# Conversion steps regrouped by slot, and the first units' exchanged x moved to transfers, in a threshold-attention and bilinear-FFN kernel

## The chip, the cores and the metric

The kernel runs on one core of a Trainium2 chip. The metric is the device time of one execution in microseconds (us). A core has a matrix engine (TensorE, PE in the profile, with PEld for its weight loads), VectorE (DVE), ScalarE (ACT), GpSimd (POOL) and SyncE (SP). SP issues most transfers; each engine works through its own instructions in order and waits for others by semaphores.

## The reference

Eight batches of eight heads attend over 576 positions with head size 64. Scores more than tau below a row's maximum are dropped. The outputs of the heads, side by side, are the 512 columns of x, and 4608 rows of x go through a bilinear FFN.

```python
scores = scale * np.matmul(q, k.transpose(0, 1, 3, 2))          # (8, 8, 576, 576)
thresh = np.max(scores, axis=-1, keepdims=True) - tau
scores = np.where(scores >= thresh, scores, -1000000000.0)
attn = np.exp(scores - np.max(scores, axis=-1, keepdims=True))
attn = attn / (np.sum(attn, axis=-1, keepdims=True) + 1e-09)
x = np.matmul(attn, v)                                          # then (B*S, H*D) = (4608, 512)
out = ((x @ w_a) * (x @ w_b)) @ w_out                           # d_ff = 1536
```

The weights arrive as 64-bit floats. The kernel reads them as pairs of 32-bit words and makes 32-bit floats of them itself.

## The kernel before, in words

**Slots.** Heads are taken in pairs; a batch has four pairs, and there are 32. A unit is 128 query rows of a pair (the fifth unit of a pair is the tail of 64 rows). One main loop goes over `g`, one unit per slot. In batch 0 the order is different from the rest: first rows 0 to 127 of all four pairs (units of slots 0 to 3), then rows 128 to 255 (slots 4 to 7), then the others. The whole program is one order written out by this loop, and `keep_order` fixes it for every engine.

**A unit.** `scores` has TensorE multiply (L312) into two PSUM tiles, VectorE take the maximum of each (`mx`, L319) and Pool make `bias` (L320) and `thr` (L321) of them. `weigh` has ACT take the exponential (L332) and VectorE multiply by the mask and sum (L336). `reciprocal` follows. For the first eight units, `diagonals` makes diagonal matrices of the reciprocals (L362), and in the next slot `turn_pe` transposes and scales on TensorE in two products: the main part (L374), which ACT copies out (L376), and the tail (L380), which ACT copies out too (L382). For these eight units, `weighted_unit`, two slots after the unit, multiplies with v (L449) and joins two halves into x (`xT`, L438 on ACT and L439 on VectorE). From slot 8 on, units are normalised on ACT (L355), transposed in blocks on VectorE (L401) and turned by a round trip through memory instead.

**The exchange.** The FFN needs x also with its two groups of 64 partitions swapped, `xS`. `exchange` (L459) copies it: on VectorE for the first eight units, on Pool for all later blocks.

**The FFN.** It runs as a generator in blocks of 256 rows; `advance` issues a number of its columns per portion of a slot (`PACE_EARLY` until slot 8, `PACE` after). A block has six steps `f` with w_a and w_b (L530) of 256 columns each, then the products with w_out (L550). The first block is ready piecemeal: its steps 0 and 1 are split into halves of 128 columns. A step is issued only when `state["converted"]` weight pieces are there and, in the first block, `state["rows"]` units of x.

**Weight conversion.** The weights are 36 pieces of 128 by 512: 24 of w_a and w_b, then 12 of w_out. `load_weights` keeps up to five raw pieces (512 KB each) loaded, in buffers of the tag "xT", of which there are seven and which x shares. A piece takes six operations:

| function | engine | line | what |
|---|---|---|---|
| convert_first | ACT | L213, L214 | absolute value of the upper word; scaling of the lower word |
| convert_clamp | POOL | L220 | clamp to the range |
| convert_sign | DVE | L226 | sign bit of the upper word joined into the lower part; frees the raw buffer |
| convert_shift | DVE | L232 | shift left by 3 |
| convert_add | POOL | L237 | integer addition of both parts |

`early[g]` lists the pieces that slot `g` starts: two each, three in slots 4 to 9. The first of a slot and the others ("late") are treated differently, by `of`: the first goes through first and clamp after the masks, sign after the normalisation or diagonals, and shift at the slot's end, and is added at the top of the next slot. The late ones start at the slot's end, are clamped and signed before the masks of the next slot, and shifted and added after its reciprocal. So on VectorE the six steps of a slot lie in four places, and on Pool the additions in two.

**Start.** SP first loads tau, from which VectorE makes five scalars (L270 to L275), then rows of q (k's on ACT's queue), raw weights and v. The rows lie in two buffers of tag "tb" (9 KB per partition) and two of tag "xT". In slots 0 to 2 `prep_pe` transposes them on TensorE (L296) and `prep_copy` copies them out (L301). Tag "tb" is needed again from slot 9, by the blocks of L401.

Of the kernel before, what the change touches and what calls it, by code (L numbers as in the profile page):

```python
# [11 lines left out]
U32 = mybir.dt.uint32  # L12
# [12 lines left out]
XT_BUFS = 7  # L25
# [25 lines left out]
def kernel(  # L51
# [36 lines left out]
    nc = tc.nc  # L88
    B, H, S, D = q.shape
    P = 128  # L90
    Q = 32
    DM = H * D
    DFF = w_a.shape[1]
    HP = H // 2
    NT = 4
# [84 lines left out]
    NPIECES = len(pieces)  # L180
    raws, stages = {}, {}
    state = {"loaded": 0, "converted": 0, "rows": 0}

    def load_weights(limit, engine=nc.sync):

        while len(raws) < limit and state["loaded"] < NPIECES:
            n = state["loaded"]
            raw = work.tile([P, CW, 2], U32, tag="xT", bufs=XT_BUFS, name="raw")
            src = pieces[n][1]
# [44 lines left out]
    def convert_add(n):  # L234
        if n in stages:
            top, low = pieces[n][0].bitcast(I32), stages.pop(n).bitcast(I32)
            nc.gpsimd.tensor_tensor(top, top, low, op=ALU.add)  # L237
            state["converted"] = n + 1


    scalars = const.tile([P, 8], FP32, name="scalars")
    tau_sb = scalars[:, 5:6]
    nc.sync.dma_start(tau_sb, tau.to_broadcast([P, 1]))
    rooms = []
# [7 lines left out]
    load_rows(1, "q", rooms[2])  # L252
    load_rows(1, "k", rooms[3], nc.scalar)
    load_weights(2)
    load_rows(2, "q", rooms[4])
# [109 lines left out]
    def turn_pe(i, u):  # L365
# [12 lines left out]
        for j, w in enumerate(ws):  # L378
            c = MAIN * (1 - j)
            nc.tensor.matmul(tp[TAIL * j:TAIL * (j + 1)], w[:, c:c + TAIL], dg[:, j],  # L380
                             start=True, stop=True)
        nc.scalar.copy(wT[:, NT], tp)  # L382

# [77 lines left out]
    def exchange_blocks():  # L461
        while complete:
# [4 lines left out]
            blocks.append(((x, xs), what))  # L467

    def weighted_unit(i, u):

# [5 lines left out]
        join(x_of[b, 0][:, hp, u * P:(u + 1) * P], pv[:, 0], pv[:, 1])  # L476
        exchange(x_of[b, 0], state["xs"], hp, u * P, (u + 1) * P, nc.vector)
        if hp == HP - 1:
            state["rows"] = u + 1
            if u == 0:  # L480
                blocks.append(((x_of[b, 0], state["xs"]), ("first", b, 0)))

# [22 lines left out]
    def ffn(xT, what):  # L505
# [7 lines left out]
        if kind == "first":  # L513
            steps = [(f, c, c + P) for c in (0, P) for f in range(n)] + steps[n:]
        for f, c0, c1 in steps:
# [110 lines left out]
    for g in range(NPIECES):  # L626
        size = min(3 if 4 <= g < 10 else 2, NPIECES - n)
        early[g] = list(range(n, n + size))
        n += size
    def of(g, late):  # L630

        return early.get(g, [])[1:] if late else early.get(g, [])[0:1]

    for g in range(len(units) + PV_LAG):
# [12 lines left out]
        if 2 <= g < BY_PE + 2:  # L647
            weighted_unit(*units[g - 2])
            running["owed"] -= (NSLOT + 1) // 2 * P
        for n in of(g - 1, False):  # L650
            convert_add(n)
        for n in of(g - 1, True):
            convert_clamp(n)
        if g < 3:
            prep_copy(*prep_pe(g + 1, "q"))
        for n in of(g - 1, True):
            convert_sign(n)
        load_weights(5 if g < 10 else 4)
        if g > BY_PE and g <= len(units):
# [13 lines left out]
        if g > BY_PE:  # L673
            advance(PORTIONS[1] * pace)
            n = g - PV_LAG
            if BY_PE <= n < len(units) and part(*units[n]):
                make_room()
                weighted(*part(*units[n]))
                running["owed"] -= (NSLOT + 1) // 2 * width(*part(*units[n]))
        for n in of(g, False):  # L680
            convert_first(n)
            convert_clamp(n)
        if here:
            reciprocal(i, u, nc.scalar if converting else nc.vector)
        for n in of(g - 1, True):
            convert_shift(n)
        for n in of(g - 1, True):
            convert_add(n)
        if here and g < BY_PE:
            diagonals(i, u)  # L690
        elif here:
            normalise(i, u)
        for n in of(g, False):
            convert_sign(n)
        load_weights(5 if g < 10 else 4)
# [8 lines left out]
        advance((PORTIONS[2] if g > BY_PE else sum(PORTIONS[:3])) * pace)  # L704
        for n in of(g, True):
            convert_first(n)
        for n in of(g, False):
            convert_shift(n)
        advance(PORTIONS[3] * pace)
# [37 lines left out]
```

## Time and profile before

| what | us |
|---|---|
| median of 3 runs | 1541.02 (1540.39 to 1543.94) |
| the profiled execution | 1543.14, span 1541.0 |
| PE busy in the span | 1484.0 (96%) |
| DVE busy | 878.4 (57%) |
| ACT busy | 590.0 (38%) |
| POOL busy | 261.6 (17%) |

The profile is of one execution. Busy is the time in which an engine worked on something; PE's ends are modelled, so a busy PE need not be at its peak. PE's granted clock (PEclk) is given in tenths or as a share of full speed. In groups, "x36" is a count, and the time in brackets is idle time of the engine ahead of an instruction, with what ended it. A matmul of 32-bit floats is recorded as two. The conversion of weights lies in the first 165 us of the span.

### The profile page before, as it was taken

What the parts mean: (1) busy time and instruction counts of PE and PEld (TensorE: products, weight loads), DVE (VectorE), ACT (ScalarE), POOL (GpSimd) and SP (SyncE); (2) the same over time, 40 slices, a digit from 0 to 9 for tenths busy, and PEclk for the clock granted to TensorE, in tenths of its full rate; (3) what the DMA queues carried; (4) which work ended last, traced back from release to release, by engine and by line L of the source; (5) the groups of instructions that cost most, each with busy time, mean ns of one, the idle gap of its engine ahead of it and who ended that gap; (6) DMA issues with size and microseconds to landing.
All of it is one profiled execution on the core that took longest, in us unless ns stands there. A gap on an engine that the chain in (4) does not pass through costs nothing.

```text
span 1541.0 us, 51117 instructions
## 1 busy us (share of the span) xinstructions
PE 1484.0 (96%) x22640; PEld 1145.4 (74%) x22640; DVE 878.4 (57%) x1844; ACT 590.0 (38%) x935; POOL 261.6 (17%) x662
## 2 busy tenths in 40 slices
PE   5778999999999999999999999999999999999998
PEld 3666786675777576778777787877777879798886
DVE  5999676567656765665545754576645665510010
ACT  4767354334433443443323433344433443410000
POOL 2666211101110111020100101011110111110000
PEclk8889999999999999999999999999999999999999
DMA  9658888679868876795547966588748876430000
GB/s 202 150 139 226 173 174 194 163 152 188 192 148 155 185 182 150 147 193 133 123 100 145 190 149 138 119 173 177 171 95 159 182 173 125 123 84 15 2 15 15
DMA packets 624557, 220.38 MB, mean 143 GB/s; under 512 B 542928, under 2 KB 612048, under 8 KB 624336
## 3 DMA queue, kind: packets, MB, share of 16 engines
q1 hardware_dynamic: 621968, 216.52, 64.1%
q8 instruction: 178, 2.92, 0.8%
q10 hardware_dynamic: 2368, 0.59, 0.2%
q14 instruction: 43, 0.35, 0.1%
HBM read 127.40 MB, written 89.65 MB: 141 GB/s over the span
## 4 chain that ended last, share of the span: by engine, by line
PE 88%; DVE 5%; SPq 2%; ACT 1%; issue 1%; DMA 1%; POOL 0%; POOLq 0%; DVEq 0%; ACTq 0%
PE pab L530 45%; PE po L550 24%; PE pv L449 9%; PE sc L312 9%; DVE low L226 1%; SPq L140 1%; DVE w L336 1%; DVE mx L319 1%; SPq L411 1%; DMA raw<-in_moe_w_b_dram 0%; PE tp L374 0%; DVE tb L401 0%; SPq L423 0%; DVE wb_sb L232 0%; DVE wo_sb L232 0%
## 5 line engine op out<-in xcount | busy, mean ns | idle before, releaser
L550 PE MATMUL po<-wo_sb,h 64*64 64x512 f32 x3456 | 424.3, 589 | 0.0
L550 PEld LDWEIGHTS po<-wo_sb,h 64*64 64x64 f32 x3456 | 222.8, 133 | 137.6 <-issue 79.7
L319 DVE TENSOR_REDUCE mx<-sc 128x1 f32<-128x576 f32 x288 | 205.0, 748 | 201.4 <-PE sc L312 201.2
L332 ACT ACTIVATE w<-sc,bias,scalars 128x576 f32<-128x576 f32 x288 | 226.8, 827 | 190.2 <-POOL bias L320 178.7
L312 PE MATMUL sc<-kT,qT 64*64 64x288 f32 x2304 | 264.1, 412 | 21.5 <-DVE w L336 9.8
L530 PE MATMUL pab<-xS,wa_sb 64*64 64x256 f32 (+1 forms) x3520 | 278.7, 376 | 3.3 <-POOL xS L459 3.3
L530 PE MATMUL pab<-xS,wb_sb 64*64 64x256 f32 (+1 forms) x3520 | 279.4, 377 | 2.5 <-issue 2.5
L355 ACT ACTIVATE w<-w,rcp 128x576 f32<-128x576 f32 x272 | 197.7, 768 | 182.9 <-DVE rcp L349 182.7
L320 POOL TENSOR_SCALAR bias<-mx,scalars 128x1 f32<-128x1 f32 x288 | 85.5, 297 | 1050.3 <-DVE mx L319 624.5
L530 PE MATMUL pab<-xT,wb_sb 64*64 64x256 f32 (+1 forms) x3136 | 250.9, 377 | 0.5 <-DVE h L538 0.5
L530 PE MATMUL pab<-xT,wa_sb 64*64 64x256 f32 (+1 forms) x3136 | 243.4, 373 | 4.4 <-DVE xT L439 3.5
L336 DVE SCALAR_TENSOR_TENSOR w<-sc,thr,w 128x576 f32<-128x576 f32 x288 | 222.4, 804 | 20.5 <-ACT w L332 17.8
L530 PEld LDWEIGHTS pab<-xS,wa_sb 64*64 64x64 f32 x3520 | 193.4, 134 | 33.6 <-POOL xS L459 9.8
L530 PEld LDWEIGHTS pab<-xS,wb_sb 64*64 64x64 f32 x3520 | 196.5, 135 | 27.9 <-issue 3.1
L312 PEld LDWEIGHTS sc<-kT,qT 64*64 64x64 f32 x2304 | 148.2, 134 | 71.6 <-issue 18.3
L530 PEld LDWEIGHTS pab<-xT,wa_sb 64*64 64x64 f32 x3136 | 170.4, 133 | 30.4 <-DVE xT L439 3.8
L530 PEld LDWEIGHTS pab<-xT,wb_sb 64*64 64x64 f32 x3136 | 173.5, 135 | 24.4 <-DVE h L538 1.1
L449 PE MATMUL pv<-wT,vm 64*64 64x320 f32 (+3 forms) x2592 | 186.1, 382 | 1.9 <-ACT h L536 1.4
L401 DVE STREAM_TRANSPOSE tb<-w 128x576 f32<-128x576 f32 x240 | 171.3, 752 | 1.3 <-ACT w L355 1.3
L449 PEld LDWEIGHTS pv<-wT,vm 64*64 64x64 f32 x2592 | 138.8, 134 | 37.3 <-issue 7.4
L538 DVE TENSOR_TENSOR h<-h,pab 128x512 f32<-128x512 f32 (+1 forms) x110 | 72.8, 662 | 125.3 <-PE pab L530 124.8
L536 ACT COPY h<-pab 128x512 f32<-128x512 f32 (+1 forms) x110 | 63.2, 574 | 203.9 <-PE pab L530 203.1
(59 smaller groups left out, 747.9 us busy)
## 6 DMA issues: line engine op xcount, KB each, us to landing
swap<-tb SPq DMA_DIRECT2D x240, 288.0 KB, 5.3
wT<-swap SPq DMA_DIRECT2D x28, 1440.0 KB, 7.4
wT<-swap SPq DMA_DIRECT2D x32, 1152.0 KB, 6.4
vm<-in_v_dram SPq DMA_DIRECT2D x32, 288.0 KB, 4.5
swap<-tbt SPq DMA_DIRECT2D x128, 72.0 KB, 2.6
out_dram<-osb SPq DMA_DIRECT2D x32, 256.0 KB, 4.0
qm<-in_q_dram SPq DMA_DIRECT2D x112, 72.0 KB, 3.5
km<-in_k_dram SPq DMA_DIRECT2D x112, 72.0 KB, 4.4
```

Source lines behind the costliest of these rows:

```text
L312: nc.tensor.matmul(sc[j if u < NT else 0][to, c], qT[r, q0:q0 + D], kT[r, c * SH:(c + 1) * SH], start=True, stop=True)
L319: nc.vector.tensor_reduce(mx[:, c], sc[j], axis=AX.XY, op=ALU.max)
L320: nc.gpsimd.tensor_scalar(bias[:, c], mx[:, c], e_nscale, None, op0=ALU.mult)
L332: nc.scalar.activation(w.rearrange("p (c k) -> p c k", c=2), s, AF.Exp, bias=bias[:, j:j + 1], scale=e_scale)
L336: nc.vector.scalar_tensor_tensor(out=wv, in0=s, scalar=thr[:, j:j + 1], in1=wv, op0=ALU.is_ge, op1=ALU.mult, accum_out=sums[:, j:j + 1])
L355: nc.scalar.activation(w, w, AF.Copy, scale=rcp[:, j:j + 1])
L401: nc.vector.transpose(tb[:, j * NB:(j + 1) * NB, (u % 2) * Q:(u % 2 + 1) * Q], w.rearrange("p (n e) -> p n e", e=Q))
L449: nc.tensor.matmul(pv[j * D:(j + 1) * D, r], vm[rows, k0], wT[rows, k0], start=(s == (NT if j == r else 0)), stop=(s == NT - 1))
L530: nc.tensor.matmul(pab[c * D:(c + 1) * D, r], w[rows, f // n, k, fs + c * D:fs + (c + 1) * D], moving, start=(k == 0), stop=(k == H - 1))
L536: nc.scalar.copy(ht, pab)
L538: nc.vector.tensor_tensor(ht, ht, pab, op=ALU.mult)
L550: nc.tensor.matmul(po[c * D:(c + 1) * D, r], ht[rows, t0:t0 + D], wo_sb[rows, F, :], start=(F == 0), stop=(F == NF - 1))
```

## The change

Five edits, all in the part of the program that belongs to the first slots.

1. Conversion by whole slots: signs of all pieces that the slot before started, then their shifts, stand at one place between the maxima and the masks; the additions follow at once on Pool, the last piece's first. ACT's and Pool's first two operations of a slot's pieces stand after the masks, one piece ahead of the reciprocal and the others after the normalisation.
2. The first units' exchange is listed in `weighted_unit` and done by two transfers per unit on SP, after the normalisation and ahead of the slot's second weight load. `state["rows"]` and the first block's start are set there.
3. The tail of `wT` is copied by VectorE and not by ACT.
4. In slot 3 the two "tb" buffers serve as four more raw buffers, each once.
5. The first block's steps 0 to 3, not 0 and 1, come in halves of 128 columns; and tau is loaded after the first rows.

```diff
@@ load_weights
-        while len(raws) < limit and state["loaded"] < NPIECES:
+        while (len(raws) < limit or extra) and state["loaded"] < NPIECES:
             n = state["loaded"]
-            raw = work.tile([P, CW, 2], U32, tag="xT", bufs=XT_BUFS, name="raw")
+            if len(raws) < limit:
+                raw = work.tile([P, CW, 2], U32, tag="xT", bufs=XT_BUFS, name="raw")
+            else:
+                raw = extra.pop(0)
@@ convert_add
-            state["converted"] = n + 1
+            state["converted"] += 1
@@ start
-    nc.sync.dma_start(tau_sb, tau.to_broadcast([P, 1]))
...
     load_rows(1, "k", rooms[3], nc.scalar)
+    nc.sync.dma_start(tau_sb, tau.to_broadcast([P, 1]))
     load_weights(2)
@@ turn_pe
-        nc.scalar.copy(wT[:, NT], tp)
+        nc.vector.tensor_copy(wT[:, NT], tp)
@@ new, and weighted_unit
+    exchanges = []
+
+    def exchange_dma():
+        while exchanges:
+            x, xs, hp, c0, c1 = exchanges.pop(0)
+            for r in range(2):
+                nc.sync.dma_start(xs[r * D:(r + 1) * D, hp, c0:c1], x[(1 - r) * D:(2 - r) * D, hp, c0:c1])
+            if hp == HP - 1:
+                state["rows"] = c1 // P
+                if c0 == 0:
+                    blocks.append(((x, xs), ("first", 0, 0)))
...
-        exchange(x_of[b, 0], state["xs"], hp, u * P, (u + 1) * P, nc.vector)
-        if hp == HP - 1:
-            state["rows"] = u + 1
-            if u == 0:
-                blocks.append(((x_of[b, 0], state["xs"]), ("first", b, 0)))
+        exchanges.append((x_of[b, 0], state["xs"], hp, u * P, (u + 1) * P))
@@ ffn
-            steps = [(f, c, c + P) for c in (0, P) for f in range(n)] + steps[n:]
+            steps = [(f, c, c + P) for c in (0, P) for f in range(2 * n)] + steps[2 * n:]
@@ main loop, top of the slot (after weighted_unit)
-        for n in of(g - 1, False):
-            convert_add(n)
-        for n in of(g - 1, True):
-            convert_clamp(n)
         if g < 3:
             prep_copy(*prep_pe(g + 1, "q"))
-        for n in of(g - 1, True):
+        for n in early.get(g - 1, []):
             convert_sign(n)
+        for n in early.get(g - 1, []):
+            convert_shift(n)
+        for n in early.get(g - 1, [])[-1:] + early.get(g - 1, [])[:-1]:
+            convert_add(n)
+        if g == 3:
+            for _ in range(2):
+                t = work.tile([P, 2 * NB, 2 * Q], U32, tag="tb", bufs=2, name="raws")
+                t = t.rearrange("p n e -> p (n e)")
+                extra += [t[:, c:c + 2 * CW].rearrange("p (f w) -> p f w", w=2) for c in (0, 2 * CW)]
         load_weights(5 if g < 10 else 4)
@@ main loop, after the masks
-        for n in of(g, False):
+        for n in early.get(g, [])[:1]:
             convert_first(n)
             convert_clamp(n)
         if here:
             reciprocal(i, u, nc.scalar if converting else nc.vector)
-        for n in of(g - 1, True):
-            convert_shift(n)
-        for n in of(g - 1, True):
-            convert_add(n)
         if here and g < BY_PE:
             diagonals(i, u)
         elif here:
             normalise(i, u)
-        for n in of(g, False):
-            convert_sign(n)
+        for n in early.get(g, [])[1:]:
+            convert_first(n)
+            convert_clamp(n)
+        exchange_dma()
         load_weights(5 if g < 10 else 4)
@@ main loop, end of the slot
-        for n in of(g, True):
-            convert_first(n)
-        for n in of(g, False):
-            convert_shift(n)
```

More of the change, by code (lines that the diff above doesn't have):

```diff
@@ L180 @@
     NPIECES = len(pieces)
-    raws, stages = {}, {}
+    raws, stages, extra = {}, {}, []
     state = {"loaded": 0, "converted": 0, "rows": 0}
     def load_weights(limit, engine=nc.sync):
-        while len(raws) < limit and state["loaded"] < NPIECES:
+        while (len(raws) < limit or extra) and state["loaded"] < NPIECES:
             n = state["loaded"]
-            raw = work.tile([P, CW, 2], U32, tag="xT", bufs=XT_BUFS, name="raw")
+            if len(raws) < limit:
+                raw = work.tile([P, CW, 2], U32, tag="xT", bufs=XT_BUFS, name="raw")
+            else:
+                raw = extra.pop(0)
             src = pieces[n][1]
@@ L629 @@
         n += size
-    def of(g, late):
-        return early.get(g, [])[1:] if late else early.get(g, [])[0:1]
     for g in range(len(units) + PV_LAG):
```

## The prediction

> **What bounds it now.** I read the page's 40 slices first.
>
> ```profile
> PE   5778999999999999999999999999999999999998
> ...
> DVE  5999676567656765665545754576645665510010
> ...
> PEclk8889999999999999999999999999999999999999
> ```
>
> TensorE is full from the fifth slice on; only the first four (about 154 us) have slack, and VectorE is at 9 there. So a change to the first 165 us is worth what it takes from TensorE's gaps there. The stage view, cut at the slots' maxima (slots 6, 7, 8; `g` in the code), shows one kind of slot:
>
> ```profile
> 67.40:79.30 11.90, 9.57 (x156) 8.25 (x158) 10.11 (x18) 7.00 (x14) 7.80 (x9) 0.71 0.56 135
> 79.30:91.20 11.90, 8.65 (x157) 7.44 (x148) 10.48 (x19) 7.66 (x16) 7.81 (x9) 0.86 0.56 136
> 91.20:101.60 10.40, 6.09 (x98) 4.67 (x96) 10.05 (x17) 7.89 (x16) 7.76 (x9) 1.00 0.62 156
> ```
>
> Columns: length, then busy PE, PEld, DVE, ACT, POOL, PE clock. VectorE has 10 of 10.4 to 11.9 us. Cut so, the time from 12 to 163.6 us holds 116.4 us of PE, so 35 us idle; each stretch times its missing clock sums to 17 more, part of it idle too. Some 45 us is the most that could come back. The timelines of VectorE and Pool in slot 6 say what the time goes to:
>
> ```profile
> 69.46 1.27 POOL L237 TENSOR_TENSOR wb_sb<-wb_sb,low 128x512 int32<-128x512 int32 x1
> 69.61 2.68 DVE L226 SCALAR_TENSOR_TENSOR low<-raw,low 128x512 uint32<-128x512 uint32 x2
> ...
> 70.70 1.05 POOL L220 TENSOR_SCALAR wa_sb<-wa_sb 128x512 f32<-128x512 f32 x1
> ...
> 71.72 1.04 POOL L220 TENSOR_SCALAR wb_sb<-wb_sb 128x512 f32<-128x512 f32 x1
> 72.22 0.80 DVE L336 SCALAR_TENSOR_TENSOR w<-sc,thr,w 128x576 f32<-128x576 f32 x1
> ```
>
> Two signs (L226) take 2.68 us beside Pool; two alone take 1.27 (slot 10, next). Mask L336 stays at 0.80 beside a clamp.
>
> ```profile
> 114.76 1.27 DVE L226 SCALAR_TENSOR_TENSOR low<-raw,low 128x512 uint32<-128x512 uint32 x2
> ...
> 114.93 1.17 POOL L320 TENSOR_SCALAR bias<-mx,scalars 128x1 f32<-128x1 f32 x1 [0.30 <-DVE mx L319]
> ```
>
> The timeline of slot 2 has one more stall:
>
> ```profile
> 33.49 0.78 DVE L459 COPY xS<-xT 64x128 f32<-64x128 f32 x2 [4.83 <-PE tp L296]
> ```
>
> VectorE's copy into xS waits 4.83 us until TensorE has read the rows that lay in that buffer.
>
> **What the Trainium skill says.** "SBUF — State Buffer", section "Who interferes with whom": VectorE and GpSimd share a port pair as an exclusive lock, taken by VectorE in two-port modes or with two SBUF inputs; the later one waits out the other. The trace agrees (steps from start to start; durations are 0.08 longer): sign 0.60 alone, 1.67 behind an add; shift (L232) 0.33 alone, 1.42 behind one; the mask, with one input in PSUM, is never longer. "TensorE: Matmul & The Clock Gate", section "What's actually happening": after an idle window of about 3.4 us the array runs at half clock. Agrees: after 3.52 us idle at 103.3, 32 matmuls of 128 columns take 1.71 us for some 5 us, then 0.88. "DMA: Bandwidth & Descriptors", section "Queues, rings and completion order": SP's transfers use one ring per DMA engine, consumed in order; so an exchange stands behind weight loads. No trace line here shows an exchange by transfer.
>
> **The parts.** A slot converts two pieces, or three in slots 4 to 9.
>
> *Signs and shifts between maxima and masks.* L226 is 38.6 us for 36, alone 36 x 0.60 = 21.6; L232 is 29.4 for 36, alone 36 x 0.33 = 11.9. The last piece's addition comes first on Pool and waits for the last shift, so no addition meets these steps; additions (1.27 alone) then run beside masks and maxima. Up to 34.5 us leaves VectorE. What can still collide: late clamps of the slot before, each costing at most 0.6.
>
> *Exchange by transfers.* Removes 16 copies, 5.4 us, and the 4.83 us stall. Adds 16 transfers of 32 KB on SP's queue, two of about 0.6 us issue per slot, waiting for xT (VectorE, long done), ahead of the second weight load. SP has that time. Landing: the nearest row, 72 KB, takes 2.6 to 4.0 us; behind one slot's 1.5 MB at about 200 GB/s up to 8.
>
> *Tail copy of wT to VectorE.* ACT loses 8 x 0.28 = 2.2 us; VectorE gains 8 of about 0.2 (0.27 for L439 with as many elements), after the masks, while it waits for scores: nothing, at most 0.3 a slot if the tail matmul is late and holds the reciprocal.
>
> *Extra raw buffers in slot 3.* Six pieces are issued together, 3 MB, some 15 us of transfers. Nobody needs them early; their cost is that slot 5's exchange queues behind them.
>
> *FFN order.* Steps f=2,3 get a first half. Two 128-column groups take 1.75 us, one of 256 takes 1.73: free. Before, the first halves run out at 2 half-steps and PE waits (3.52 us in slot 9, then half clock). PACE_EARLY gives 2050-640 = 1410 columns a slot, 0.69 half-step of 2048, so 2.75 by slot 8 and 4.1 after slot 9: the four first halves last until the second ones' rows are there.
>
> *tau after the rows.* Row transfers start 0.4 us sooner, but tau gates VectorE's first copy (scalars L270 to L275, 0.6 us). Tau landed 3.3 us after issue; now issued at about 4.5 it lands near 8, its six steps end near 8.6, and qT comes at 8.6, not 8.33. Bounds -0.4 and +2.4; I take +0.3.
>
> **Slots, step by step** (from the slot's first maximum). Two pieces, slots 3 and 4: maxima 1.34, xT to 2.0 (PE pv 1.3, ACT 0.27, VectorE 0.27), signs and shifts 1.86, masks 1.5, next scores 1.2 and 0.3 of semaphores: 7.0, in slot 4 with ACT's third piece 7.4, against 8.9 and 8.0: **-2.5**.
>
> Slot 2: without the stall qT, two signs, two shifts, masks end at 32.6; k's transposes then end at 33.5, kT at 34.3 instead of 37.7, and its scores start on a warmer PE: **-4.0** (3.4 to 4.5).
>
> Three pieces: VectorE alone would cycle in 7.8. Pool: bias and thr 1.1, additions 3.8, clamps 1.8, plus waiting 2.0+2.8 for the last shift, then bias 1.8 us late in the next slot: 8.75. PE in order: pv 1.3, tp behind xT 2.0 to 4.1, its copies on ACT to 5.2, tail 5.7, pab 0.69 x 3.5 = 2.6, scores 1.0 and the maxima's start: 9.7. So PE's chain is what is late next: slots 6 and 7 take 9.7 each, against 11.9: -4.4. Slot 5 is 7.8 by VectorE and PE (its pab is not yet there at its start) plus a wait of pab for xS, 0 to 3.5, I take 1.5: 9.3 against 10.4: -1.1. Together **-5.5**. Slot 8: 9.7 against 10.4; slot 9, no longer starved: 9.2 against 11.8: **-3.3**. FFN after slot 9 is 4.1 half-steps, before about 3.4: 0.7 x 3.5 = **-2.5** later.
>
> Slots 10 to 15: VectorE's 7.75 (two pieces, transposes) becomes about 6.8, but PE's share is 3446 columns, 5.9 us, plus scores 1.0. Only idle time can go: 1.5 at 127, 3.1 at 152, half clock after it 2.5; I take **-4** of these. From 165 us on PE is full: nothing.
>
> Sum: -2.5-4.0-5.5-3.3-2.5-4.0+0.3 = **-21.5**. The profiled execution took 1543.1 (span 1541.0), so 1521.6; against the median of 1541.0, **1519.5**. Bounds: Pool and PE never late -33 (1508), half of it lost -11 (1530).
>
> **Rivals.** *A new in-order chain eats most (1532).* Pool's block of three additions and three clamps, the exchange behind 3 MB, and pab ahead of scores make slots 5 to 9 take 11: these bring about 1 us in place of 8.8, slots 10 to 15 bring 2, leaving -2.5-4-1-2+0.3 = -9.2. For it: Pool would be busy 6.7 of 8.75. Against: before, PE ended its pab 1.1 to 1.4 us ahead of VectorE in slots 6 and 7.
>
> *Slower: the bias starves (1551).* If Pool gets the port only after the whole run of signs and shifts, exps start 2.8 us late. The 1.17 us bias above, which ends just after two signs, speaks for it; the 1.05 us clamps, which alternate with signs, against. Run 2.8, bias 0.3, exps 1.6, masks 1.5, tail 0.45, pab 2.6, scores 1.0, first maximum 0.75, xT 0.7 give 11.7, with a cold PE 12.8, in six slots +1.7, in seven two-piece slots +0.6, less 4 in slot 2: +10. It decides where a slot's first bias, not only the second, starts after the shifts.
>
> *It changes nothing (1540).* The collisions merely move: additions into the next slot's signs. Against: Pool's 5.6 us from the last shift end before those.
>
> **Numbers.** Main case 0.68 (1508 to 1528), eaten 0.18 (1528 to 1537), slower 0.08, nothing 0.06. A measurement of this kernel tells about 0.3%, 4.6 us, from no change. Faster 0.86, same 0.06, slower 0.08. Range 1508 to 1535.
>
> **What would show it.** L226 near 0.68 each and L232 near 0.41 for nearly all 36, additions near 1.27; no L459 on VectorE; slot 3's maximum about 4 us earlier than 40.1, slot 10's near 97 instead of 113.4; no wait of pab for xT. Wrong if signs are still above 1 us, if exps wait over 2 us for bias, or if pab waits over 4 us for xS.

## The result, and the profile after

The changed kernel takes 1534.17 us, median of 4 runs (1532.87 to 1535.89), against 1541.45 us (1540.39 to 1543.94) for the kernel before beside it: a ratio of 0.9951, 95% interval 0.9934 to 0.9968. On the chip of the last experiments it was 0.9962 (0.9949 to 0.9974). So it is faster by some 6 to 7 us, under half a per cent and a third of the 21.5 us forecast. Its profiled execution took 1535.89, with a span of 1534.1. From the conversion steps to the function `exchange`, lines of the changed kernel have the numbers of before plus 3 (L226 is now L229, L439 now L442); the exchange by transfers is L478, the FFN's w_a and w_b products L541, its evictions L547 (ACT) and L549 (VectorE).

The 40 slices of the page:

```profile
PE   5778999999999999999999999999999999999998
...
DVE  5667576666656765674545754576555764510010
...
PEclk9999999999999999999999999999999999999999
```

VectorE's first digits fell from 9 to 6 or 7; its busy time fell from 878.4 to 848.6 us. The clock row lost its three 8s. But the PE row is the same digit for digit.

The stages of slots 6, 7 and 8 (length, busy PE, PEld, DVE, ACT, POOL, clock, DMA share, GB/s):

```profile
63.30:72.70 9.40, 7.50 (x170) 6.54 (x166) 6.80 (x17) 6.66 (x14) 5.30 (x8) 0.97 0.52 121
72.70:83.60 10.90, 7.72 (x171) 6.41 (x166) 6.79 (x16) 7.78 (x16) 8.28 (x11) 1.00 0.47 104
83.60:92.70 9.10, 7.13 (x158) 5.83 (x149) 6.35 (x16) 6.77 (x13) 7.09 (x8) 1.00 0.60 134
```

VectorE has 6.4 to 6.8 us a slot where it had over 10, and no longer fills the slot. The timeline of slot 6 shows why:

```profile
65.25 1.89 DVE L229 SCALAR_TENSOR_TENSOR low<-raws,low 128x512 uint32<-128x512 uint32 x3
67.06 0.42 DVE L235 TENSOR_SCALAR wb_sb<-wb_sb 128x512 uint32<-128x512 uint32 x1
...
68.07 0.81 DVE L339 SCALAR_TENSOR_TENSOR w<-sc,thr,w 128x576 f32<-128x576 f32 x1
68.23 2.51 POOL L240 TENSOR_TENSOR wb_sb<-wb_sb,low 128x512 int32<-128x512 int32 x2 [2.84 <-DVE wb_sb L235]
```

Three signs take 1.89 us where two took 2.68; Pool's additions wait for the last shift and then run beside the masks at 1.26 each.

Where the time came from and went, by the times of the slots' first maxima (a slot lasts from its own to the next one's). The column "again" is another profiled execution of the changed kernel (span 1535.2):

| term of the forecast | before, us | forecast | measured | again |
|---|---|---|---|---|
| start, slots 0 and 1 | 27.06 | +0.3 | +0.8 | +2.0 |
| slot 2 | 13.06 | -4.0 | -4.6 | -3.0 |
| slots 3 and 4 | 16.87 | -2.5 | -4.8 | -3.7 |
| slot 5 | 10.45 | -1.1 | +4.4 | +2.1 |
| slots 6 and 7 | 23.75 | -4.4 | -3.4 | -3.8 |
| slots 8 and 9 | 22.23 | -3.3 | -0.2 | -0.2 |
| slots 10 to 15 | 50.22 | -4.0 | +2.8 | +3.3 |
| from slot 16 on | 1377.4 | -2.5 | -2.0 | -2.5 |
| sum (spans) | 1541.0 | -21.5 | -6.9 | -5.8 |

Up to slot 5's start the change had gained 8.5 us in the first execution, more than the 6.2 forecast, and 4.7 in the second. The second has two stretches of 3.41 us at half clock in slots 1 to 3, the first has none there; so the length of a slot in one execution is uncertain by some 2 us. Slot 5 and slots 8 to 15 gave the shortfall. TensorE's idle time over the span hardly moved, 57.0 to 55.1 us (span less busy PE); what went is missing clock, from about 20 to 9 us (the span times what the mean granted clock, 0.987 and 0.994, lacks to 1).

### The profile page after: what moved, and what is told of

Read it like the earlier page. It is cut to its first block, busy times and chain, and to the rows that moved or that the text cites. A ratio compares the mean times of both kernels' runs of the same rounds, so it can differ in the third digit from the quotient of the medians.

```text
span 1534.1 us, 51632 instructions
## 1 busy us (share of the span) xinstructions
PE 1479.0 (96%) x22896; PEld 1116.3 (73%) x22896; DVE 848.6 (55%) x1838; ACT 588.1 (38%) x929; POOL 260.7 (17%) x662
## 4 chain that ended last, share of the span: by engine, by line
PE 89%; DVE 3%; DMA 2%; ACT 2%; SPq 1%; issue 1%; POOL 1%; DVEq 0%; POOLq 0%; ACTq 0%
PE pab L541 46%; PE po L561 23%; PE sc L315 9%; PE pv L452 9%; PE tp L377 1%; DVE mx L322 1%; DVE tb L404 1%; SPq L414 1%; SPq L426 0%; DMA wT<-swap 0%; ACT low L217 0%; SPq L140 0%; DVE low L229 0%; DMA swap<-tb 0%; DMA raw<-in_moe_w_a_dram 0%
## 5 line engine op out<-in xcount | busy, mean ns | idle before, releaser
L541 PE MATMUL pab<-xS,wa_sb 64*64 64x256 f32 (+1 forms) x3584 | 278.9, 372 | 5.0 <-POOL xS L462 3.3
L541 PE MATMUL pab<-xS,wb_sb 64*64 64x256 f32 (+1 forms) x3584 | 279.6, 372 | 0.0
L323 POOL TENSOR_SCALAR bias<-mx,scalars 128x1 f32<-128x1 f32 x288 | 89.8, 317 | 1041.3 <-DVE mx L322 625.2
L541 PE MATMUL pab<-xT,wb_sb 64*64 64x256 f32 (+1 forms) x3200 | 249.7, 371 | 5.5 <-DVE h L549 3.9
L541 PE MATMUL pab<-xT,wa_sb 64*64 64x256 f32 (+1 forms) x3200 | 244.9, 369 | 3.8 <-POOL thr L324 2.1
L541 PEld LDWEIGHTS pab<-xS,wa_sb 64*64 64x64 f32 x3584 | 188.6, 133 | 40.2 <-POOL xS L462 9.7
L541 PEld LDWEIGHTS pab<-xS,wb_sb 64*64 64x64 f32 x3584 | 190.9, 134 | 29.6 <-issue 1.0
L315 PEld LDWEIGHTS sc<-kT,qT 64*64 64x64 f32 x2304 | 145.0, 135 | 67.2 <-issue 12.4
L541 PEld LDWEIGHTS pab<-xT,wb_sb 64*64 64x64 f32 x3200 | 169.5, 134 | 32.1 <-DVE h L549 4.3
L541 PEld LDWEIGHTS pab<-xT,wa_sb 64*64 64x64 f32 x3200 | 167.1, 133 | 33.7 <-issue 3.1
L452 PEld LDWEIGHTS pv<-wT,vm 64*64 64x64 f32 x2592 | 132.3, 133 | 46.8 <-issue 9.2
L549 DVE TENSOR_TENSOR h<-h,pab 128x512 f32<-128x512 f32 (+1 forms) x112 | 73.2, 654 | 132.5 <-PE pab L541 128.6
L547 ACT COPY h<-pab 128x512 f32<-128x512 f32 (+1 forms) x112 | 63.6, 568 | 204.3 <-PE pab L541 203.6
```

Source lines behind the costliest of these rows:

```text
L315: nc.tensor.matmul(sc[j if u < NT else 0][to, c], qT[r, q0:q0 + D], kT[r, c * SH:(c + 1) * SH], start=True, stop=True)
L323: nc.gpsimd.tensor_scalar(bias[:, c], mx[:, c], e_nscale, None, op0=ALU.mult)
L452: nc.tensor.matmul(pv[j * D:(j + 1) * D, r], vm[rows, k0], wT[rows, k0], start=(s == (NT if j == r else 0)), stop=(s == NT - 1))
L541: nc.tensor.matmul(pab[c * D:(c + 1) * D, r], w[rows, f // n, k, fs + c * D:fs + (c + 1) * D], moving, start=(k == 0), stop=(k == H - 1))
L547: nc.scalar.copy(ht, pab)
L549: nc.vector.tensor_tensor(ht, ht, pab, op=ALU.mult)
```

## The experiments

All times are against the kernel before on the same chip. "Slot 5" and the like are lengths between first maxima of the profiled execution.

**Clamps later.** Theory: from slot 9 on, Pool's late clamps hold up the next slot's bias.

```diff
@@ top of the slot, ahead of the signs
+        for n in early.get(g - 1, [])[1:]:
+            convert_clamp(n)
@@ after the normalisation
         for n in early.get(g, [])[1:]:
             convert_first(n)
-            convert_clamp(n)
```

> The changed kernel, with the clamps of a slot's second and third piece issued on Pool at the top of the next slot, behind that slot's bias and thr, and no longer at the end of their own slot ahead of them. Theory A (the bias waits behind a clamp that waits for ACT's late piece, so exps, the FFN's evictions on ACT and then TensorE come late in slots 11 to 15): the first bias of slots 11, 13, 14 and 15 starts within 1.5 us of the slot's first maximum instead of 1.5 to 2.8; TensorE's wait of 3.67 us for ACT's h near 148 falls below 1.5; 3 to 5 us faster than the changed kernel, 1529 to 1531. Theory B (the late landing of the exchange in slot 5 is the loss): slot 5 stays near 14.9 us, and the time within 1 us of 1534. Theory C (the additional 128-column halves call for evictions that stand behind the bunched steps): waits near 100 and 119 stay, and the time falls by less than 1.5.

Measured: 1543.11 us, 1.0007 (1.0001 to 1.0014). All that the change gained is gone: slots 9 to 15 take 71.4 us, not 66.0, although the first bias now begins within 1.13 us of every slot's maximum (in the change up to 3.0). A timeline line shows what the move costs:

```profile
123.73 0.43 DVE L235 TENSOR_SCALAR wo_sb<-wo_sb 128x512 uint32<-128x512 uint32 x1 [0.77 <-POOL wo_sb L223]
```

The shift now waits for the clamp, and the transposes, evictions and masks stand behind the shift. The theory's remedy fails, and it brings a cost of its own: a longer run of conversions on VectorE costs TensorE at once (waits of 2.78 and 2.23 us for VectorE at 117.65 and 125.86).

**The exchange earlier.** Theory: slot 5 is long because the transfers are issued late.

```diff
@@ top of the slot, after weighted_unit
+            if g > 2:
+                exchange_dma()
```

> The changed kernel, with the exchange transfers of slots 3 to 9 issued on SP at the top of the slot, right after the join into x and ahead of both weight loads of that slot. Theory B: pab no longer waits for xS in slot 5 and stays at full clock; slot 5 falls from 14.9 us to 11 to 12, and the time by 2.5 to 4, to 1530 to 1532. Theory A or C: slot 5 shortens, but ACT's three pieces and Pool's late bias hold the next slots, and the time falls by less than 1.

Measured: 1535.63 us, 0.9954 (0.9942 to 0.9966). Slot 5 fell to 11.4 us, without a wait for xS, and yet the end is where it was, since slots 0 to 2 took 2.8 us more in this execution and slots 9 to 15 did not move (66.3). Beside the second execution of the change, whose slots 0 to 2 took as long, slot 5 is only 1.1 us shorter.

**Two first halves, as before.** Theory: halves of 128 columns double the evictions on ACT and VectorE.

```diff
-            steps = [(f, c, c + P) for c in (0, P) for f in range(2 * n)] + steps[2 * n:]
+            steps = [(f, c, c + P) for c in (0, P) for f in range(n)] + steps[n:]
```

> The changed kernel, with only the first block's steps 0 and 1 in halves of 128 columns, as before the change. Theory C: fewer evictions in slots 8 to 12, TensorE's waits from 94 to 120 us (8.0 us in five) fall by half, 1 to 3 us faster, 1531 to 1533. Theory A or B: the halves are a gain in themselves, TensorE runs out of them in slot 8 and waits for the second unit's rows, then runs at half clock: 2 to 5 us slower, 1536 to 1539.

Measured: 1537.67 us, 0.9965 (0.9952 to 0.9977), no faster. Slots 11 and 12 fell from 9.6 and 8.0 to 7.4 and 7.5 us, as the theory has it. But in slot 9 TensorE's timeline has a new wait:

```profile
100.36 0.87 PE L541 MATMUL pab<-xS,wa_sb 64*64 64x128 f32 x8 [6.73 <-DMA xS<-xT]
```

With two steps the first halves run out in slot 9, and the second unit's exchange, issued late in that slot, is not there. So the four steps of halves do cover a late operand, and pay for it in evictions.

**tau first again.**

```diff
+    nc.sync.dma_start(tau_sb, tau.to_broadcast([P, 1]))   # ahead of the rows again
...
-    nc.sync.dma_start(tau_sb, tau.to_broadcast([P, 1]))
```

> The changed kernel, with tau loaded first, as before the change. If the start only shifts what follows: the first maximum 1.1 us earlier (12.4 instead of 13.5), and the end 1.0 to 1.4 us earlier, near 1533. If the later slots absorb it (slot 5 waits for transfers, which do not come earlier): within 0.5 us of the changed kernel.

Measured: 1536.98 us, 0.9968 (0.9956 to 0.998). The first maximum comes at 12.40 instead of 13.49, but slot 5 takes 17.8 us, and the end is no sooner.

**Shifts and additions behind the masks** from slot 9 on, signs left in place.

```diff
+        if g <= BY_PE:
             for n in early.get(g - 1, []):
                 convert_shift(n)
             for n in early.get(g - 1, [])[-1:] + early.get(g - 1, [])[:-1]:
                 convert_add(n)
...
             weigh(i, u)
+        if g > BY_PE:
+            for n in early.get(g - 1, []):
+                convert_shift(n)
+            for n in early.get(g - 1, [])[-1:] + early.get(g - 1, [])[:-1]:
+                convert_add(n)
```

> The changed kernel; from slot 9 on the shifts and additions stand behind the masks, and only the signs stay between maxima and masks, so that the block ahead of masks and FFN evictions on VectorE is 1.2 to 1.8 us and not 1.9 to 2.8. Theory C (in slots 9 to 15 the FFN's evictions and the masks stand behind the block on VectorE, and TensorE, with four PSUM buffers, waits for them): slots 9 to 15 take 62 to 64 us together instead of 66.0, TensorE's waits there fall from 14.1 us to 10 or less, and the time falls by 2 to 3.5 us against the changed kernel. Theory E (what sets these slots is ACT's own chain of exps, normalisation and late pieces): the additions come later on Pool and delay the bias, and the time is the same or up to 2 us longer.

Measured: 1535.43 us, 0.9954 (0.9937 to 0.9971), no different from the change. TensorE's wait in slot 9 fell from 2.49 to 1.48 us and that slot from 13.0 to 10.4, but slot 10 grew from 8.7 to 11.3, 1.1 us of it a wait for xS by a transfer.

**Each main part alone**, in the kernel before. First the conversion order, edit 1 of the change (here its core, with the removals of the change's diff):

```diff
+        for n in early.get(g - 1, []):
+            convert_sign(n)
+        for n in early.get(g - 1, []):
+            convert_shift(n)
+        for n in early.get(g - 1, [])[-1:] + early.get(g - 1, [])[:-1]:
+            convert_add(n)
```

Then the exchange by transfers, edit 2:

```diff
-        exchange(x_of[b, 0], state["xs"], hp, u * P, (u + 1) * P, nc.vector)
+        exchanges.append((x_of[b, 0], state["xs"], hp, u * P, (u + 1) * P))
...
+        exchange_dma()
         load_weights(5 if g < 10 else 4)
```

> The kernel before, with the regrouping of the conversion steps alone: exchange on VectorE, tail copy on ACT, tau first, no additional raw buffers, halves for steps 0 and 1 only. Signs near 0.68 and shifts near 0.41. Theory C: slots 3 to 8 get shorter by 6 to 9 us together, slots 9 to 15 longer by 2 to 5, slot 2 keeps its stall of 4.8 us: 1536 to 1539, against 1541 to 1542.6 of the kernel before. If the lock's price was all: slots 9 to 15 shorter too, 1530 to 1533.

> The kernel before, with the exchange of the first eight units by transfers alone. Slot 2 loses its stall (4 us shorter), VectorE 5.4 us of copies. If the transfer's late landing matters by itself: slot 5 longer by 1 to 3 us, and slot 9's wait for the second unit's rows grows from 3.5 to 5 or more: 1538 to 1541. If it is only late behind the additional raw loads of slot 3, which are not here: no wait for xS over 1 us, 1535 to 1537.

Measured: conversion order alone 1537.55, 0.9961 (0.9947 to 0.9975); exchange alone 1538.71, 0.9971 (0.996 to 0.9981). With the conversion order alone, slot 2 keeps its stall and takes 15.6 us; with the exchange alone it takes 10.1. With the exchange alone slot 5 takes 13.5 us, 3.9 of it a wait for xS. So each part does what was forecast of it where it was aimed, and the exchange brings its wait along, here without the extra raw buffers (in slot 9 it is another 3.96 us). Slots 11 to 15 have 4.8 us of idle PE in the kernel before, 4.1 with the conversion order alone, 4.3 with the exchange alone, 8.5 in the changed kernel, 3.9 with two first halves: the extra idle time there does not come without the longer halves. Whether they cost as much without the bunched conversions no run shows. The two parts' gains, added, would make 0.993; the change has 0.995, so the rest of it, or what the parts do to each other, may have cost some 3 us, which is near the noise. Of the rest, the copy of `wT` by VectorE was not run alone.

**Two edits together.** The earlier exchange gained nothing at the end and the two halves lost; if the two hide each other's wait, both together (the second and the third diff above) should gain.

> The changed kernel with the exchange's transfers issued at the top of the slot, right behind the join into xT, and with first halves for two FFN steps as before. If two separate costs ate the gain (the late exchange in slots 5 and 9, where the two-step order alone lost 6.7 us to a wait for xS, and the doubled evictions of the 128-column steps in slots 11 and 12, where the two-step order alone needed 7.4 us a slot), both go: slot 5 is 11.4 us, slots 9 and 10 take 19 to 22 together, slot 16 starts near 153, the time is 1528 to 1530. Rival: the idle time of TensorE only moves, because FFN work of the first units runs out whatever the order: slot 16 starts near 158 and the time stays at 1534 to 1538, as for each edit alone.

Measured: 1531.68 us, 0.9926 (0.9912 to 0.994). Slot 16 starts at 153.8 us, not at 158.7 (158.6 and 158.4 with either edit alone), and from there on it takes 1376.0 us, the change 1375.4: the same. In place of the wait of 6.73 us for xS stands one of 0.74; the other, for xT, is there with two first halves alone, too:

```profile
92.37 0.45 PE L541 MATMUL pab<-xT,wa_sb 64*64 64x128 f32 x8 [2.41 <-DVE xT L442]
94.21 1.08 PE L541 MATMUL pab<-xS,wa_sb 64*64 64x128 f32 x6 [0.74 <-DMA xS<-xT]
```

The forecast of 153 held; that of slot 5 (11.4) did not: it took 14.9. By length most of the gain lies in slots 6 to 8 (26.0 us, the change 29.4), where fewer first halves are issued. Slots 9 to 15 take up that work and still need 65.6 us in place of 66.0, with 8.4 us of idle PE in place of 14.1. The first bias of slots 9 and 12 to 14 is as late here as 2.5 to 3.7 us after the maximum, and yet TensorE idles less than in the change, so a late bias is not what made the change slow.

**Earlier exchange and later shifts**, again two of the diffs above.

> The changed kernel with the exchange's transfers at the top of the slot and, from slot 9 on, shifts and additions behind the masks. If the two waits are separate (late xS in slot 5, 3.5 us; masks behind the bunch of conversions in slot 9, 2.7 us, which alone came back as a wait of 1.1 us for xS in slot 10), slots 5 and 9 to 10 lose about 5 us together and the time is 1529 to 1531. Rival: idle only moves, 1534 to 1536.

Measured: 1533.8 us, 0.9947 (0.9931 to 0.9963). Slot 5 takes 11.8, slots 9 and 10 take 22.7, one more than in the change, and slots 11 to 15 keep 9.2 us of idle PE. The gains do not add up while the long halves stay.

**The exchange on ACT's queue.**

```diff
-                nc.sync.dma_start(xs[r * D:(r + 1) * D, hp, c0:c1], ...)
+                nc.scalar.dma_start(xs[r * D:(r + 1) * D, hp, c0:c1], ...)
```

> The changed kernel with the same 16 transfers at the same place in program order, but issued on ScalarE's queue. If they are late because they stand on SP's queue behind weight loads (issue behind a load that waits for a sign, and landing behind its bytes), the waits of pab for xS in slot 5 (1.7 us) fall below 0.5 and slot 5 shortens by 2 to 3.5 us, as with the issue at the slot's top. If the transfer itself is what takes long, the waits stay. In either case ScalarE pays two issues a slot in slots 2 to 9. By the rival that idle only moves, the time is within 2 us of the changed kernel's 1534 to 1536.

Measured: 1543.01 us, 1.0003 (0.9994 to 1.0011): the whole gain is gone. Slot 5 takes 19.7 us, with this wait in it:

```profile
67.61 0.73 PE L541 MATMUL pab<-xS,wa_sb 64*64 64x128 f32 x6 [6.11 <-DMA xS<-xT]
```

ACT reaches the issue only at 60.68, behind its own exponentials, copies and conversions of slot 5, and the transfer lands 6.9 us later, though it has no load ahead of it on its queue. (The median from issue to landing is 4.4 us.) A queue of its own does not make it fast.

**Copies by VectorE in place of the transfers**, between signs and shifts.

```diff
             convert_sign(n)
+        exchange_dma()
@@ exchange_dma
-                nc.sync.dma_start(xs[r * D:(r + 1) * D, hp, c0:c1], x[(1 - r) * D:(2 - r) * D, hp, c0:c1])
+                nc.vector.tensor_copy(xs[r * D:(r + 1) * D, hp, c0:c1], x[(1 - r) * D:(2 - r) * D, hp, c0:c1])
```

> The changed kernel with the exchange done by VectorE's copies again (two of 0.34 us a slot, between signs and shifts) instead of transfers; all else as changed. If the transfers are what lengthened slot 5 and what slots 9 and 10 wait for, slot 5 falls to 11 to 12 us, the waits for xS by a transfer vanish and slots 9 to 15 take 62 to 64 us in place of 66.0; VectorE's 0.7 us a slot and a stall in slot 2 for the rows' reads give back up to 7 us, so the time is 1530 to 1536. If the halves and the bunch of conversions are what fills slots 9 to 15, these stay at 66 or more and the time is 1536 to 1540.

Measured: 1540.21 us, 0.9978 (0.9969 to 0.9988). Slot 5 falls to 10.3 us and no wait for xS is left, but slots 6 to 8 take 31.7 (29.4 in the change) and slots 9 to 15 68.0. On the whole the transfers are worth having.

**Without the extra raw buffers**, on top of the two edits together.

```diff
-        if g == 3:
-            for _ in range(2):
-                t = work.tile([P, 2 * NB, 2 * Q], U32, tag="tb", bufs=2, name="raws")
-                t = t.rearrange("p n e -> p (n e)")
-                extra += [t[:, c:c + 2 * CW].rearrange("p (f w) -> p f w", w=2) for c in (0, 2 * CW)]
```

> The kernel with the exchange at the slot's top and first halves for two steps, without the four extra raw buffers of slot 3. If the bytes of the weights that these let load at once (six pieces, 3 MB, slots 3 to 5) are what keeps the exchange's transfers of slot 4 from landing for 5 us, the median from issue to landing falls to about 2.3, pab waits under 0.5 us for xS in slot 5, and slot 5 takes 11 to 12 us in place of 14.9; slot 16 starts at 151 to 153. Rival: slot 5's end lies near 62 to 64 us whatever is done to the transfers (it did in every kernel so far but two), and without the extra buffers pieces come later: slots 6 to 8 lengthen by 1 to 3 us and the time is 1532 to 1537.

Measured: 1530.03 us, 0.9923 (0.9911 to 0.9935), equal to the two edits within the intervals. The line from issue to landing of the four transfers issued from 46 to 60 us, with the two edits and then without the buffers as well:

```profile
DMA to landing us min/median/max: 6.8/8.0/9.3
```

```profile
DMA to landing us min/median/max: 1.9/2.2/2.9
```

So the 3 MB that the extra buffers let load at once are what made these transfers slow. They do not explain the others. The same line for those issued after 72 us, when the 3 MB have long landed, first of the change, which issues them between a slot's loads, then of the two edits, which issue them ahead of both:

```profile
DMA to landing us min/median/max: 5.0/5.5/6.3
```

```profile
DMA to landing us min/median/max: 1.8/1.9/2.2
```

Slot 5 falls to 11.4 us, without a wait for xS. That the buffers had lengthened it is not shown: it begins at 52.6 us here and at 47.4 with the two edits, and two kernels that keep the buffers and begin it near 51 (the earlier exchange, alone and with later shifts) need 11.4 and 11.8, without that wait too. Nothing later suffers: slots 6 to 8 take 25.9, as with the buffers.

**The join on VectorE**, on top of the two edits: the copy of L441 moves from ACT to VectorE for the first eight units.

```diff
@@ join, when called by weighted_unit
-        nc.scalar.copy(out, lo)
+        nc.vector.tensor_copy(out, lo)
```

> The kernel with the exchange at the slot's top and first halves for two steps, with both halves of the join into xT of the first units on VectorE, none on ScalarE. If ScalarE's third piece, which stands ahead of the join in its order, is what starts slot 5's delay (the join's copy began at 51.26 us though its products were there at 49.5), xT is there 1.4 us sooner in slot 5, the exchange lands sooner by as much, slot 5 shortens by 1 to 2 us and slot 9's wait of pab for xT (2.4 us) falls below 1; the time is 1529 to 1531. If the chain through the clamp, the bias and the exps on Pool and ScalarE decides, pab in slot 5 starts no sooner and slot 5 stays within 0.5 of 14.9; VectorE's extra 0.3 us a slot then costs up to 2 us in slots 6 to 9: 1531 to 1534.

Measured: 1530.99 us, 0.9925 (0.9912 to 0.9937), as fast as the two edits. Slot 5 takes 10.5 us and the wait of slot 9 for xT falls from 2.41 to 0.29, but 3.44 us of waiting for xS come in its place, and slot 4 grows from 6.4 to 8.3:

```profile
45.10 2.01 POOL L323 TENSOR_SCALAR bias<-mx,scalars 128x1 f32<-128x1 f32 x2
```

```profile
46.78 1.55 ACT L335 ACTIVATE w<-sc,bias,scalars 128x576 f32<-128x576 f32 x2 [1.80 <-POOL bias L323]
```

With no step of ACT in front of VectorE's signs, Pool's two biases, 0.29 each when alone, take 2.01 us (the first 1.65), and the exponentials wait.

**The changed kernel beside these.**

> The changed kernel itself, beside the others on one chip: 1534 to 1536, 0.995 of the kernel before. By the theory that two waits cover for each other, the kernel with both edits is 3 to 5 us faster than this one; by the theory that idle only moves, they are equal within 2 us.

Measured: 1536.08 us, 0.9962 (0.9949 to 0.9974), an interval that lies wholly above those of the last two kernels. Two halves, the exchange at the slot's top and no extra raw buffers beat both the kernel before and the change, by 12 and 6 us; the buffers' share in that is within the noise (0.9923 without them, 0.9926 with them).

## Why the prediction was right, and where it failed

**The direction was right, and so was what VectorE gets back; the sum was not.** A third of the 21.5 us came. 1534.17 lies at the slow end of the range of 1508 to 1535, outside the main case (1508 to 1528, given 0.68) and in the time of the rival "a new in-order chain eats most" (1528 to 1537, given 0.18). What failed is the price of the work that comes next in order once VectorE is free: slot 5, put at 9.3 us and measured at 14.9 and 12.5, and the FFN in slots 8 to 15, put at 7.3 us less and measured at 2.6 and 3.1 more.

**Signs and shifts: right.** L229 is 0.69 us each (forecast 0.68) and L235 0.42 (0.41), for all 36; additions are 1.27. VectorE got back 15.3 us of signs and 14.9 of shifts, 30.2 of the "up to 34.5". Slots 3 and 4 gained more than forecast because I put the next scores after both masks (1.2 us and 0.3). In slot 3's timeline the scores start at 40.62, as the first mask ends, and VectorE idles for only 0.21 us between the second mask's end at 41.44 and the next maximum at 42.01:

```profile
39.91 0.80 DVE L339 SCALAR_TENSOR_TENSOR w<-sc,thr,w 128x576 f32<-128x576 f32 x1
...
40.62 1.34 PE L315 MATMUL sc<-kT,qT 64*64 64x288 f32 x16 [0.85 <-ACT wT L379]
```

**Slot 2: right.** The stall went, and the two executions lie on both sides of -4.0 (-4.6 and -3.0). The parts alone show that the exchange did it.

**Slots 6 and 7: nearly right.** 9.36 and 10.97 us against 9.7 each (in which pab's 0.69 x 3.5 is 2.4, not 2.6). That TensorE's own chain comes to be late next was right: slot 7's maximum waits 2.06 us for scores, at 72.68.

**Slot 5: the term that failed first.** I wrote "7.8 by VectorE and PE (its pab is not yet there at its start) plus a wait of pab for xS". The pab that is not there at the start stands in PE's order after the slot's turns and ahead of the next scores, so the slot has the full chain of 9.7. The rest can be read from the timelines of slot 5, of Pool, of ACT and of PE:

```profile
50.86 0.61 POOL L223 TENSOR_SCALAR wa_sb<-wa_sb 128x512 f32<-128x512 f32 x1 [0.53 <-ACT wa_sb L216]
51.45 1.05 POOL L323 TENSOR_SCALAR bias<-mx,scalars 128x1 f32<-128x1 f32 x2
```

```profile
51.77 1.60 ACT L335 ACTIVATE w<-sc,bias,scalars 128x576 f32<-128x576 f32 x2 [0.27 <-POOL bias L323]
53.27 1.06 ACT L379 COPY wT<-tp 128x512 f32<-128x512 f32 x2
```

```profile
54.43 1.10 PE L541 MATMUL pab<-xT,wa_sb 64*64 64x128 f32 x32 [2.12 <-POOL thr L324]
...
56.96 1.36 PE L541 MATMUL pab<-xS,wa_sb 64*64 64x128 f32 x16 [1.21 <-DMA xS<-xT]
58.78 0.86 PE L541 MATMUL pab<-xS,wa_sb 64*64 64x128 f32 x8 [0.47 <-DMA xS<-xT]
59.27 2.09 PE L541 MATMUL pab<-xT,wb_sb 64*64 64x128 f32 x32
60.97 2.30 PE L315 MATMUL sc<-kT,qT 64*64 64x288 f32 x16
```

The slot's maximum began at 48.45, but the bias stands behind a clamp that waited for ACT's third piece, so it begins at 51.45. Exponentials and ACT's copy of wT follow; the copy ends at 54.33, and pab begins 0.1 later. (The profile names `thr`, which had ended at 54.01. That the copy is what pab waited for is read from the times: in all thirteen profiled executions of the changed kernel and its variants pab begins 0.1 us after it.) Then pab waits 1.21 and 0.47 us for xS, and after the gaps 32 matmuls take 2.09 us instead of 1.05. The late bias itself cost little: pab begins 5.98 us after the maximum, and the chain of 9.7 has it at 5.7. In numbers: 9.7, 1.7 of waits for xS and 3.1 of missing clock are 14.5 of the measured 14.87; in the second execution 9.7, 0.5 and 1.7 are 11.9 of 12.51. The wait for xS was forecast (1.5); the full chain and the half clock were not. The Trainium skill, "TensorE: Matmul & The Clock Gate", section "What's actually happening", says that the activity window that decides the clock is free-running, so that the moment at which the clock changes depends on where in the window the matmuls fall. The runs agree: behind the same gap of 2.12 us the first 32 matmuls took 1.10 us in the change's first profile and 1.98 in its second.

**Slots 8 to 15: the term that failed by most.** Two sentences of the forecast were wrong. The first: two 128-column groups for one of 256 are "free". They are on TensorE (1.75 against 1.73 us), but each brings its own eviction by ACT and its own product by VectorE, on engines that have a conversion bunch in these slots. Slot 9 of the change shows one such product:

```profile
98.82 1.43 DVE L404 STREAM_TRANSPOSE tb<-w 128x576 f32<-128x576 f32 x2
...
100.17 0.38 DVE L549 TENSOR_TENSOR h<-h,pab 128x256 f32<-128x256 f32 x1
100.48 0.80 DVE L339 SCALAR_TENSOR_TENSOR w<-sc,thr,w 128x576 f32<-128x576 f32 x1
100.61 1.27 PE L541 MATMUL pab<-xT,wb_sb 64*64 64x128 f32 x32 [2.49 <-DVE h L549]
```

L549 stands behind signs, shifts and transposes; it ends at 100.55, and pab, which needs the PSUM buffer that it frees, starts at 100.61, 2.49 us late. From slot 9 to slot 15 TensorE has seven such waits for h or a mask of more than 1 us, 12.8 us in all. In the kernel before there are two, besides the 3.52 us for x in slot 9:

```profile
127.49 0.67 PE L312 MATMUL sc<-kT,qT 64*64 64x288 f32 x2 [1.47 <-DVE w L336]
152.38 0.67 PE L312 MATMUL sc<-kT,qT 64*64 64x288 f32 x2 [3.10 <-DVE w L336]
```

Two first halves take them out of slots 11 and 12. The lengths hide part of this loss: in slots 6 to 8 the change issues 2.1 half-steps of the FFN, the kernel before 1.4, so that slots 9 to 15 have less to do and yet take 4 us more, with 14.1 us of idle PE in place of 7.0. The second: that half of the idle time of slots 10 to 15, "-4", would come back since VectorE has less to do. The two waits for masks did go, but the forecast followed no chain through these slots, and TensorE now waits 3.67 us for ACT's h in slot 14. Slot 10's first maximum came at 105.7 us, not near 97. That the four first halves last until the second unit's rows are there, so that nothing starves in slot 9, was right; the runs with two halves show what it is worth (6.73 us) and that an earlier exchange does the same for less.

**FFN ahead: right in number, by luck.** -2.0 and -2.5 against -2.5. At slot 10's start the change has done 4.2 half-steps and the kernel before 3.8 (forecast 4.1 and 3.4). But at slot 16's start both have done all products of the first block with w_a and w_b, and of those with w_out the kernel before 25 recorded matmuls, the change 22: the lead is gone. What went after slot 16 is one gap of TensorE, which of all sixteen profiled executions only that of the kernel before has, and which ended with nothing that the profile shows:

```profile
1206.43 1.24 PE L530 MATMUL pab<-xS,wb_sb 64*64 64x256 f32 x17 [2.48 <-issue]
```

**tau: direction right, size low.** The scalars waited until 9.14 us for tau, not 8, and the first maximum came 1.1 us late; the run with tau first shows that slot 5 takes that up.

**The rivals.** "A new in-order chain eats most" gave 1532 and slots 5 to 9 of 11 us each; they took 11.5 and 10.9 on average. That its exchange lands late behind 3 MB is shown; that this cost the time is not, since the earlier exchange took the wait away and the end stayed. Nor is its Pool block: moving clamps out of the way made things worse. It also let slots 10 to 15 gain 2, where they lost 3. The starving bias exists (0.48 us on average, 0.35 before), but it did not decide. What stays open: why slot 5 ends between 62.0 and 64.8 us in eleven of the executions, though it starts anywhere from 46.9 to 52.7; a wait for xS or a half-speed array filled it in all but one (the copies by VectorE, where the slot starts last), and I have not shown that one thing sets it.

## What to carry to other kernels

When an engine is relieved, price the next chain in order of issue through the whole slot, with its evictions and the copy that frees its buffer, not only the operation that was freed. A transfer that replaces a copy inherits the queue's and the DMA engines' load: issue it ahead of the loads of its time, and look at what is loading in those microseconds before adding a prefetch that nobody needs yet. A term that comes out right can still be luck: count the work that it speaks of. Two edits can hide each other's cost, so try them in pairs: here the earlier exchange brought nothing and the shorter halves lost, and together they gained 4 to 5 us.

## What the runs showed of the hardware

- A transfer of 32 KB between two SBUF tiles took 1.8 to 2.2 us from issue to landing where it was issued ahead of a slot's weight loads (the two edits, from slot 6 on), 5.0 to 6.3 where it was issued between them (the change, slots 7 to 9), and 6.8 to 9.3 while six pieces (3 MB) loaded at once (the two edits, slots 4 and 5). Issued on another engine's queue beside the same loads it took 4.4 in the median.
- Pool's tiny instructions lose most to a run of VectorE's conversions: two biases took 2.01 us instead of 0.58 where signs and shifts followed each other without a gap. The Trainium skill, "SBUF — State Buffer", section "Who interferes with whom", says that whoever issues first holds the shared pair for the whole instruction; here the wait outlasted more than one VectorE instruction (the first bias took 1.65, a sign is 0.68).
- Half clock does not need one unbroken idle stretch: idle gaps of 0.4 and 2.12 us with 0.44 us of work between them were followed at once by half clock in six of ten profiled executions; in three it came after a third gap of 1.0 to 1.2 us, in one not at all. Two stretches of the change, the second at half clock (length, busy PE, clock, DMA share, GB/s):

```profile
53.63:57.04 3.41, 1.41 (x42) 1.00 1.03 216
57.04:60.45 3.41, 2.94 (x46) 0.50 0.58 146
```

From 14 to 175 us half clock always lasted 3.41 us or a multiple of it. It began 77 times in the sixteen profiled executions, each time behind 3.41 us in which PE was busy for at most 1.92. Cut in step with that, 526 stretches at full clock held more, and none of them was followed by half clock; of 112 that held no more, 35 were not either.
